# Making the Strassen operands of x inside the buffers that the first group multiplies from

## The chip, the cores and the metric

The kernel runs on one core of a Trainium2 chip. The metric is the device time of one execution in microseconds (us); three runs of the kernel before took 867.95, 872.8 and 872.8 us, median 872.8. Engines are named as in the profile: PE (TensorE), DVE (VectorE), ACT (ScalarE), POOL (GpSimd), SP (SyncE, which issues DMAs).

## The reference

```python
def _attn_ref(q, k, v):                       # q, k, v: (4, 8, 576, 64) float32
    gamma = 1.0 - 2.0 ** (-5.0 - np.arange(H))
    Dmat = np.where(rel >= 0, gamma[:, None, None] ** rel, 0.0)     # rel = i - j
    return np.matmul(scale * np.matmul(q, k.transpose(0, 1, 3, 2)) * Dmat, v)
def _moe_ref(x, w_in, w_out):                 # w_in (512, 2048), w_out (2048, 512)
    h = x @ w_in
    return np.maximum(0.01 * h, h) @ w_out
def _moe2_ref(x, w_in, w_out):
    h = np.maximum(x @ w_in, 0.0)
    return h * h @ w_out
# reference: x = attention, turned to (2304, 512); then _moe_ref; then _moe2_ref
```

## The kernel before, in words

**Attention stage.** 2304 tokens are worked through as 20 chunks (four batches of five; the fifth of each is half a chunk). Per chunk PE makes the scores, DVE multiplies them by the decay mask (tile `r`, L465), PE makes the output and a running state, and ACT copies both (L506, L509). The outputs go to three tiles `ysb`, one for each block of 768 tokens. Between chunks the program issues a few steps of two other jobs: making weights (`run`, counts in `RATE`) and making operands of x (`build`, counts in `BUILD`).

**Two feed-forward layers.** A layer is four groups of 512 hidden columns (`g` = 0 to 3; below, groups 0 to 3 are layer 0, groups 4 to 7 are layer 1). A group goes over the three blocks of tokens (`p` = 0 to 2), so there are 24 blocks, called (group, p). A block has a first half, `first`: seven products a la Strassen (`product`, L274, 12 matmuls each) of weight operands with operands of x; and a second half, `second`: the product with w_out (L371), 96 matmuls in layer 0 and 72 in layer 1. Around them ACT copies PSUM (tile `s`, L300), DVE adds (L322, L336, L341), and each result is split into a rounded part (`ghi`, ACT, L307) and the rest (`glo`, DVE, L312), since one float32 matmul is made of three on rounded parts. The results of `second` are copied to `ysb` by ACT in a layer's first group (L380), and added to it by DVE in the others (L382).

**Weights.** They are prepared a group ahead: 40 steps a group (two tasks of 12 steps for w_in, two of 8 for w_out), each step one or two instructions, nearly all on DVE, on tiles `raw` and `sf`. `raw` has one buffer, loaded by SP in two DMAs (`ahead`, L111); a task begins on ACT with `exponent` (L120), which waits for that load. `pace` is called between products and sets how many steps are issued where; one unit of its clock `now` is one product, 15 to a block.

**Operands of x.** A block's seven products need seven combinations of quarters of `ysb`, each as a rounded part (ACT, L227) and the rest (DVE, L233). `operands(layer, p)` makes them with 4 subtractions on DVE (L239 to L245), and ACT's queue stores both parts to DRAM (L205). `load_x` loads them from DRAM on SP's queue (L260) into five buffers `x` (`SLOTS`), for every group. Only the first five of block (0, 0) are made in the buffers themselves. In layer 0 the operands are made in the attention stage and in block (0, 0); for layer 1, `operands(1, p)` is made in the block after (3, p).

The order of instructions on each engine is the order in which the program emits them. All engines take theirs in order.

Of the kernel before, what the change touches and what calls it, by code (L numbers as in the profile page):

```python
# [19 lines left out]
P = 128  # L20
# [6 lines left out]
HT = 384  # L27
# [22 lines left out]
def retention_ffn_kernel(ctx: ExitStack, tc: tile.TileContext, full, rows, half, halfv, w1, w2, const, mask, gk, out):  # L50
# [40 lines left out]
    class Weights:  # L91


        def __init__(self):
            self.tasks = []
            for g in range(2 * NG):
                layer, f = divmod(g * GRP, NF)
                a, b, c, d = ((j, layer, f + 2 * u) for j in range(2) for u in range(NU))

                self.tasks += [a, c, d, b] if g else [a, b, c, d]  # L100
            self.raws, self.loads = [], 0

        def ahead(self):

            if self.loads < len(self.tasks):
                j, layer, f = self.tasks[self.loads]
                raw = stage.tile([P, 2, DM, 2], U32, tag="raw", bufs=RAW, name="raw")
                for i in range(2):

                    src = (w1, w2)[layer][f + i if j else f + 1 - i, j]  # L110
                    nc.sync.dma_start(raw[:, i].rearrange("p n t -> p (n t)"), src)  # L111
                self.raws.append(raw.rearrange("p i n t -> p (i n) t"))
                self.loads += 1

# [7 lines left out]
        def steps_in(self, layer, f):  # L122
# [17 lines left out]
            yield  # L140
            nc.vector.tensor_tensor(v, v, t, add)  # L141
            yield

            self.ahead()
# [17 lines left out]
        def steps_out(self, layer, f):  # L162
# [18 lines left out]
            yield  # L181
            nc.scalar.activation(hi, f32(a), AF.Copy)
            yield
            self.ahead()
# [17 lines left out]
    late = []  # L202

    def store(dst, src):
        nc.scalar.dma_start(f32(dst.rearrange("p k n -> p (k n)")), f32(src.rearrange("p k n -> p (k n)")))  # L205

    def flush():

        while late:
            layer, p, i, x, lo = late.pop(0)  # L210
            store(x[:, 1], lo)
            xd[layer, p, i] = x

    def operands(layer, p):

        x = ysb[p].rearrange("p (k t n) -> p k t n", k=NK, t=2)
        b11, b21, b12, b22 = (x[:, k : k + 2, t] for t in range(2) for k in (0, 2))

        def put(i, src):
            x = dram.tile([P, 2, 2, HT], F32R, name=f"x{layer}{p}{i}")  # L220
            if (layer, p) == (0, 0) and i < SLOTS:

                t = xs[0, 0, 0, i] = xpool.tile([P, 2, 2, HT], F32R, tag="x", name="x")
                hi, lo = t[:, 0], t[:, 1]
            else:
                hi = stage.tile([P, 2, HT], F32R, tag="xb", bufs=XB, name="xb")
            nc.scalar.activation(hi, src, AF.Copy)  # L227
            store(x[:, 0], hi)
            flush()
            yield  # L230
            if (layer, p) != (0, 0) or i >= SLOTS:
                lo = stage.tile([P, 2, HT], F32R, tag="xb", bufs=XB, name="xb")
            nc.vector.tensor_tensor(lo, src, f32(hi), sub)  # L233
            late.append((layer, p, i, x, lo))
            yield

        yield from put(0, b11)
        yield from put(1, b21)
        nc.vector.tensor_tensor(b11, b12, b11, sub)  # L239
        yield from put(6, b22)  # L240
        nc.vector.tensor_tensor(b12, b22, b12, sub)
        yield from put(4, b11)
        nc.vector.tensor_tensor(b22, b22, b11, sub)
        yield from put(3, b12)
        nc.vector.tensor_tensor(b21, b21, b22, sub)  # L245
        yield from put(2, b22)
        yield from put(5, b21)
        flush()

    uses = [(l, g, p, i) for l in range(2) for g in range(NG) for p in range(NB) for i in range(7)]  # L250
    loaded, used = [SLOTS], [0]
# [265 lines left out]
    def run(n, limit):  # L517

        while n > 0 and done[0] < limit:
            next(steps, None)  # L520
            done[0] += 1
            n -= 1

    def build(n=1):

        ran = 0
        while builds and ran < n:
            try:
                next(builds[0])
                ran += 1  # L530
            except StopIteration:
                builds.pop(0)
# [3 lines left out]
    with tc.manual_schedule():  # L536
        with tc.tile_pool(name="att", bufs=1) as pool, tc.tile_pool(name="ps_s", bufs=1, space=PSUM) as ps_s:
# [20 lines left out]
            for i in range(n):  # L558
# [12 lines left out]
                for p in range(NB):  # L571
                    a, t = tokens(i)
                    if a < (p + 1) * 2 * HT <= a + t:
                        builds.append(operands(0, p))
# [12 lines left out]
        run(GROUP, GROUP - OWN)  # L587


        whole = NB * 15  # L590
        for layer in range(2):
            for g in range(NG):
# [15 lines left out]
                built = [0]  # L608
                for p in range(NB):

# [11 lines left out]
                    if layer == 0 and g == NG - 1:  # L622
                        builds.append(operands(1, p))
# [56 lines left out]
```

## Time and profile before

| | |
|---|---|
| runs | 867.95, 872.8, 872.8 us |
| the profiled execution: its time, its span | 871.71 us, 869.9 us |
| PE busy, DVE busy, ACT busy, POOL busy | 834.7, 602.6, 343.4, 47.4 us |
| attention stage, up to the first product | 103.76 us |
| a block where PE never waits | 31.2 us (layer 0), 30.95 us (layer 1) |
| mean granted TensorE clock | 0.980 of full speed |

The profile gives, for each engine, the time in which it was busy. A view by stretches gives the same for a window of time; the length of the window stands first in its row. For a block of the feed-forward layers the window runs from its first matmul to that of the next block, so its length is the block's time.

### The profile page before, as it was taken

The numbers are of one execution on the slowest core, as the hardware profiler recorded it, in microseconds if no ns is written. First come the engines' busy times: TensorE is split into PE (matmuls) and PEld (weight loads), VectorE is DVE, ScalarE is ACT, GpSimd is POOL, SyncE is SP. The second block draws the span as 40 slices with busy tenths as digits, with TensorE's granted clock in tenths as the row PEclk, the third lists the DMA queues.
The fourth block names the chain that finished last, engine by engine and source line by source line (L and its number), as shares of the span: only waits on it lengthen the run. The fifth ranks groups of instructions, "written<-read, shape, count | busy, mean of one in ns | idle before, by whom it ended". The sixth has DMA issues, their size and how long they took to land.

```text
span 869.9 us, 12551 instructions
## 1 busy us (share of the span) xinstructions
PE 834.7 (96%) x5084; PEld 785.2 (90%) x5084; DVE 602.6 (69%) x734; ACT 343.4 (39%) x447; POOL 47.4 (5%) x36
## 2 busy tenths in 40 slices
PE   8868899999999999999998999999999999999998
PEld 7767799999999999999998988789989988998996
DVE  3898776555776576667778888576778688755534
ACT  2444565455354245235345445343333223321311
POOL 2647000000000000000000000000000000000000
PEclk9988699999999999999999999999999999999999
DMA  9999699575486467457579897766558547735831
GB/s 338 312 360 353 248 379 347 191 297 204 159 298 250 150 247 271 180 202 302 178 320 386 329 375 284 259 238 254 169 230 302 190 159 281 268 107 209 284 136 72
DMA packets 57065, 220.12 MB, mean 253 GB/s; under 512 B 6960, under 2 KB 7984, under 8 KB 57008
## 3 DMA queue, kind: packets, MB, share of 16 engines
q1 hardware_dynamic: 44912, 186.29, 58.4%
q10 hardware_dynamic: 12096, 33.04, 9.8%
q8 instruction: 40, 0.66, 0.3%
q14 instruction: 17, 0.14, 0.0%
HBM read 181.55 MB, written 37.75 MB: 252 GB/s over the span
## 4 chain that ended last, share of the span: by engine, by line
PE 74%; DVE 11%; DMA 8%; ACT 3%; issue 2%; ACTq 0%; SPq 0%; POOL 0%; DVEq 0%; POOLq 0%
PE yps L371 40%; PE a L274 20%; PE b L274 14%; DMA raw<-in_w 4%; DMA gq<-in_const 2%; DMA x<-x 1%; DVE r L465 1%; DVE xb L233 1%; DVE sf L180 1%; ACT t L283 1%; DMA mask<-in_mask 1%; ACT sf L120 1%; DMA x<-xb 1%; ACT ghi L307 1%; DVE sf L141 1%
## 5 line engine op out<-in xcount | busy, mean ns | idle before, releaser
L274 PE MATMUL a<-x,ihi 128*128 128x384 f32 x768 | 197.2, 337 | 4.5 <-ACT s L300 2.8
L274 PE MATMUL b<-x,ihi 128*128 128x384 f32 x576 | 147.0, 336 | 3.7 <-DVE t L322 2.7
L274 PEld LDWEIGHTS a<-x,ihi 128*128 128x128 f32 x768 | 139.6, 189 | 7.4 <-ACT s L300 4.1
L371 PE MATMUL yps<-ghi,ohi 128*128 128x384 f32 x384 | 128.7, 335 | 1.6 <-ACT ysb L380 0.5
L274 PE MATMUL a<-x,ilo 128*128 128x384 f32 x384 | 129.3, 337 | 0.0
L371 PE MATMUL yps<-glo,ohi 128*128 128x384 f32 x384 | 128.4, 334 | 0.6 <-DVE glo L312 0.6
L371 PE MATMUL yps<-ghi,olo 128*128 128x384 f32 x384 | 128.3, 334 | 0.0
L312 DVE TENSOR_TENSOR glo<-t,ghi 128x768 fp32r<-128x768 f32 x96 | 91.8, 956 | 47.6 <-ACT ghi L307 46.8
L382 DVE TENSOR_TENSOR ysb<-yps,ysb 128x384 f32<-128x384 f32 (+1 forms) x126 | 75.8, 610 | 62.8 <-PE yps L371 62.4
L371 PE MATMUL yps<-ohi,glo 128*128 128x512 f32 x288 | 112.3, 390 | 0.0
L371 PE MATMUL yps<-olo,ghi 128*128 128x512 f32 x288 | 112.3, 390 | 0.0
L371 PE MATMUL yps<-ohi,ghi 128*128 128x512 f32 x288 | 112.0, 389 | 0.0
L274 PEld LDWEIGHTS b<-x,ihi 128*128 128x128 f32 x576 | 103.9, 188 | 5.4 <-DVE t L322 3.3
L307 ACT ACTIVATE ghi<-t 128x768 fp32r<-128x768 f32 x96 | 81.1, 845 | 68.8 <-DVE t L285 55.4
L300 ACT ACTIVATE s<-a 128x768 f32<-128x768 f32 x48 | 39.0, 812 | 153.3 <-PE a L274 151.2
L274 PE MATMUL b<-x,ilo 128*128 128x384 f32 x288 | 96.3, 334 | 0.0
L371 PEld LDWEIGHTS yps<-ghi,ohi 128*128 128x128 f32 x384 | 72.1, 188 | 2.8 <-DVE ysb L382 1.1
L371 PEld LDWEIGHTS yps<-glo,ohi 128*128 128x128 f32 x384 | 72.1, 188 | 0.8 <-DVE glo L312 0.8
L274 PEld LDWEIGHTS a<-x,ilo 128*128 128x128 f32 x384 | 72.7, 189 | 0.0
L371 PEld LDWEIGHTS yps<-ghi,olo 128*128 128x128 f32 x384 | 72.1, 188 | 0.0
L322 DVE TENSOR_TENSOR t<-b,s 128x768 f32<-128x768 f32 x24 | 23.0, 956 | 70.2 <-PE b L274 64.0
L371 PEld LDWEIGHTS yps<-ohi,glo 128*128 128x128 f32 x288 | 54.1, 188 | 11.3
(63 smaller groups left out, 1049.3 us busy)
## 6 DMA issues: line engine op xcount, KB each, us to landing
x<-x SPq DMA_DIRECT2D x163, 768.0 KB, 6.0
raw<-in_w SPq DMA_DIRECT2D x64, 512.0 KB, 6.2
x<-xb ACTq DMA_DIRECT2D x74, 384.0 KB, 6.8
kv<-in_rows SPq DMA_DIRECT2D x16, 512.0 KB, 6.7
out<-ysb SPq DMA_DIRECT2D x18, 256.0 KB, 2.0
q<-in_full SPq DMA_DIRECT2D x16, 256.0 KB, 5.5
kt<-in_full SPq DMA_DIRECT2D x16, 256.0 KB, 5.5
x<-x ACTq DMA_DIRECT2D x10, 384.0 KB, 6.1
```

What stands on the lines that cost most here:

```text
L120: nc.scalar.activation(f32(a), f32(raw[:, :, 1]), AF.Abs)
L141: nc.vector.tensor_tensor(v, v, t, add)
L180: nc.vector.scalar_tensor_tensor(a, high, 1 << 31, a, ALU.bitwise_and, ALU.bitwise_or)
L233: nc.vector.tensor_tensor(lo, src, f32(hi), sub)
L274: nc.tensor.matmul(ps[:, u, :HT], a[:, w, s], x[:, b, k], start=(start and k == 0 and i == 0), stop=(k == 1 and i == 2), skip_group_check= ...
L283: nc.scalar.activation(t, src, AF.Prelu, alpha=0.01)
L300: nc.scalar.activation(t, ps[:, :, :HT], AF.Copy)
L307: nc.scalar.activation(h, t, AF.Copy)
L312: nc.vector.tensor_tensor(l, t, f32(gs[key][0]), sub)
L322: nc.vector.tensor_tensor(t11, b[:, :, :HT], s1, add)
L371: nc.tensor.matmul(acc, a, b, start=(j == u == i == 0), stop=(j == 1 and u == NU - 1 and i == 2))
L382: nc.vector.tensor_tensor(y, acc, y, add)
```

## The change

Seven buffers `x` stand in place of five, and the staging buffers `xb` are gone. The operands of a layer's first group are made in these buffers, in the order of use, and that group multiplies from them without a load; each is stored to DRAM whole, on SP's queue, from the same buffer (`store`, called from `pace`), and only groups 1 to 3 of a layer load them. So `operands(layer, p + 1)` is built in the second half of block (first group, p), `operands(1, 0)` in that of block (3, 2), and only `operands(0, 0)` in the attention stage. A difference that was written over b22 has a tile of its own (`t2`). The last 8 weight steps of the first group (`OWN`) move from the attention stage into block (0, 0). `ahead` is called one step earlier, and in the groups a weight task does not begin before three units of `pace` have gone by since its load was emitted (`ARRIVE`). The paces of groups 0, 3 and 4 are set by a share for each block (`SHARE`) in place of an exponent.

```diff
-SLOTS = 5
+SLOTS = 7
-XB = 5
-RATE = [1, 2, 2, 3, 3, 3] + [2] * 13 + [0]
-BUILD = [0] * 6 + [2] * 13 + [0]
+RATE = [1, 1, 2, 2, 2, 2] + [2] * 11 + [0] * 3
+BUILD = [0] * 6 + [1] * 11 + [0] * 3
-SPACE = 0.9
-BEND = {0: 1.6, NG - 1: 0.7, NG: 1.4}
-OWN = 0
+SPACE = .65
+SHARE = {0: (0.15, 0.45), NG - 1: (0.47, 0.85), NG: (0.2, 0.55)}
+OWN = 8
+LAG = 1
+ARRIVE = 3
...
         def steps(self):
             for j, layer, f in self.tasks:
+                while self.clock < self.due:
+                    yield True
                 yield from (self.steps_out if j else self.steps_in)(layer, f)
...
+    def store(use, x):
+        layer, _, p, i = use
+        d = dram.tile([P, 2, 2, HT], F32R, name=f"x{layer}{p}{i}")
+        nc.sync.dma_start(f32(d.rearrange("p a k n -> p (a k n)")), f32(x.rearrange("p a k n -> p (a k n)")))
+        xd[layer, p, i] = d
...
+        def hi(i, src):
+            use = layer, 0, p, i
+            while uses[loaded[0]] != use or loaded[0] == used[0] + SLOTS:
+                yield True
+            loaded[0] += 1
+            xt[i] = xs[use] = xpool.tile([P, 2, 2, HT], F32R, tag="x", name="x")
+            nc.scalar.activation(xt[i][:, 0], src, AF.Copy)
+        def lo(i, src):
+            t = xt[i]
+            nc.vector.tensor_tensor(t[:, 1], src, f32(t[:, 0]), sub)
+            kept.append(((layer, 0, p, i), t))
+        yield from hi(0, b11)
+        yield
+        yield from hi(1, b21)
+        lo(0, b11)
+        yield
+        lo(1, b21)
         nc.vector.tensor_tensor(b11, b12, b11, sub)
+        yield
+        nc.vector.tensor_tensor(t2, b22, b11, sub)
+        yield
+        yield from hi(2, t2)
...
-            if (l, p, i) not in xd:
+            if g == 0 or (l, p, i) not in xd:
                 break
...
+        weights.arrive = ARRIVE
...
                 def pace(now, ceiling):
-                    part = min(1, now / (whole - 3)) ** BEND.get(i, 1)
+                    into = min(1, (now - 15 * p) / (6 if busy[p] else 12 if p == NB - 1 else 15))
+                    share = (0, *SHARE.get(i, (0.36, 0.71)), 1)
+                    part = share[p] + (share[p + 1] - share[p]) * into
                     want = start + math.ceil((limit - start) * part)
-                    if builds and now >= built[0]:
-                        build()
-                        built[0] = now + SPACE
+                    while len(kept) > LAG:
+                        store(*kept.pop(0))
+                    while builds and now >= built[0] and build():
+                        built[0] = max(built[0], now - 1) + SPACE
+                    if not builds:
+                        while kept:
+                            store(*kept.pop(0))
+                    weights.clock = whole * i + now
...
                 for p in range(NB):
+                    built = [15 * p + 8]
+                    if g == 0 and p + 1 < NB:
+                        builds.append(operands(layer, p + 1))
+                    elif layer == 0 and g == NG - 1 and p == NB - 1:
+                        builds.append(operands(1, 0))
...
                     second(layer, g, p, gs, in_second)
-                    if layer == 0 and g == NG - 1:
-                        builds.append(operands(1, p))
+                    build(99)
+                weights.due = 0
+                run(GROUP, limit)
```

DVE near the end of the attention stage, from one full chunk's mask product (`r`) to the last, before (`ysb_67` is the second block of x):

```order
L465 TENSOR_TENSOR r<-scps,mask 128x1024
L172 TENSOR_SCALAR raw<-raw 128x1024
L239 TENSOR_TENSOR ysb_67<-ysb_67 128x2x384
L174 TENSOR_SCALAR sf<-sf 128x1024
L233 TENSOR_TENSOR xb<-ysb_67,xb 128x768
L465 TENSOR_TENSOR r<-scps,mask 128x1024
L176 SCALAR_TENSOR_TENSOR sf<-raw 128x1024
L241 TENSOR_TENSOR ysb_67<-ysb_67 128x2x384
L178 TENSOR_SCALAR sf<-sf 128x1024
L233 TENSOR_TENSOR xb<-ysb_67,xb 128x768
L465 TENSOR_TENSOR r<-scps,mask 64x8x64
```

and the same chunks of the change:

```order
L483 TENSOR_TENSOR r<-scps,mask 128x1024
L183 SCALAR_TENSOR_TENSOR sf<-raw,sf 128x1024
L234 TENSOR_TENSOR x<-ysb_66,x 128x768
L483 TENSOR_TENSOR r<-scps,mask 128x1024
L188 TENSOR_SCALAR sf<-sf 128x1024
L234 TENSOR_TENSOR x<-ysb_66,x 128x768
L190 SCALAR_TENSOR_TENSOR olo<-sf 128x1024
L483 TENSOR_TENSOR r<-scps,mask 64x8x64
```

Eight instructions stand between these three mask products before, five in the change; the operands of the second block are gone from the stage, and so is the last weight task (L172, L174 and so on).

SP's DMAs of the change from the end of the attention stage into block (0, 1) (`x_1028` and so on are the DRAM copies; L211 stores, L113 loads raw weights):

```order
L113 DMA raw<-in_w 128x1024 x2
L211 DMA x_1028<-x 128x1536
L211 DMA x_1030<-x 128x1536
L211 DMA x_1032<-x 128x1536
L211 DMA x_1034<-x 128x1536
L211 DMA x_1036<-x 128x1536
L211 DMA x_1038<-x 128x1536
L113 DMA raw<-in_w 128x1024 x2
L211 DMA x_1203<-x 128x1536
```

Six stores of whole operands stand one behind the other ahead of a load of raw weights. Before, SP's queue had seven loads of x in their place, and the stores were on ACT's queue, two halves for each operand.

DVE of the change in the last building block, (4, 1), from the third-last sum of its first half (`t_4778` is the difference's own tile):

```order
L359 TENSOR_TENSOR t<-b,s 128x768
L303 SCALAR_TENSOR_TENSOR t<-t 128x768
L330 TENSOR_TENSOR glo<-t,ghi 128x768 x2
L306 TENSOR_TENSOR t<-t 128x768
L330 TENSOR_TENSOR glo<-t,ghi 128x768
L234 TENSOR_TENSOR x<-ysb_68,x 128x768
L188 TENSOR_SCALAR sf<-sf 128x1024
L190 SCALAR_TENSOR_TENSOR olo<-sf 128x1024
L234 TENSOR_TENSOR x<-ysb_68,x 128x768
L244 TENSOR_TENSOR ysb_68<-ysb_68 128x2x384
L175 TENSOR_SCALAR raw<-raw 128x1024
L177 TENSOR_SCALAR sf<-sf 128x1024
```

Before, the operands of layer 1 were made in blocks (3, 1), (3, 2) and (4, 0); here those of the third block stand in (4, 1), among its weight steps.

## Rows read from the trace of the kernel before

**Rows 1.** The page: span, busy time by engine, granted clock by fortieths.
```profile
span 869.9 us, 12551 instructions
PE 834.7 (96%) x5084; PEld 785.2 (90%) x5084; DVE 602.6 (69%) x734; ACT 343.4 (39%) x447; POOL 47.4 (5%) x36
PEclk9988699999999999999999999999999999999999
```
**Rows 2.** Windows: each block that waits, two groups that don't; length first.
```profile
core 0: us, PE busy (x) PEld busy (x) DVE busy (x) ACT busy (x) POOL busy (x), PEclk, DMA share, GB/s
...
103.76:137.08 33.32, 33.32 (x181) 33.32 (x182) 21.74 (x26) 17.73 (x25) 0.00 (x0) 0.93 0.91 346
137.08:170.09 33.01, 31.77 (x181) 31.13 (x181) 20.97 (x25) 19.05 (x26) 0.00 (x0) 1.00 0.77 286
170.09:203.76 33.67, 32.06 (x182) 31.17 (x182) 18.57 (x22) 16.43 (x23) 0.00 (x0) 1.00 0.60 227
203.76:297.36 93.60, 93.60 (x542) 93.60 (x542) 60.77 (x82) 37.57 (x44) 0.00 (x0) 1.00 0.60 222
...
390.96:423.20 32.24, 31.50 (x182) 31.18 (x182) 24.20 (x33) 13.77 (x16) 0.00 (x0) 1.00 0.63 237
423.20:455.66 32.46, 31.96 (x182) 31.09 (x182) 23.09 (x28) 15.93 (x19) 0.00 (x0) 1.00 0.75 288
455.66:489.94 34.28, 32.10 (x182) 31.14 (x182) 30.89 (x43) 17.07 (x21) 0.00 (x0) 1.00 0.98 384
489.94:521.31 31.37, 31.16 (x157) 28.03 (x157) 25.40 (x32) 14.44 (x19) 0.00 (x0) 1.00 0.92 347
521.31:553.53 32.22, 31.23 (x157) 28.06 (x156) 21.67 (x24) 14.80 (x19) 0.00 (x0) 1.00 0.81 292
553.53:587.40 33.87, 31.76 (x158) 28.03 (x156) 25.39 (x30) 16.01 (x21) 0.00 (x0) 1.00 0.60 226
...
587.40:680.24 92.84, 92.84 (x470) 84.30 (x469) 70.86 (x88) 30.25 (x35) 0.00 (x0) 1.00 0.61 224
```
**Rows 3.** Timeline of block (0, 2): SP's raw load, ACT behind it, PE's stall.
```profile
177.01 0.93 SPq L111 DMA_DIRECT2D raw<-in_w  x2
...
184.96 1.12 ACT L120 ACTIVATE sf<-raw 128x1024 f32<-128x1024 f32 x1 [5.53 <-DMA raw<-in_w]
...
189.49 0.44 PE L371 MATMUL yps<-ghi,ohi 128*128 128x384 f32 x1 [0.52 <-ACT ghi L307]
```
**Rows 4.** Windows of the attention stage: sixth to twentieth mask product, and the rest.
```profile
25.91:97.02 71.11, 56.63 (x768) 49.92 (x768) 65.17 (x62) 32.75 (x59) 37.39 (x25) 0.83 0.92 331
97.02:103.76 6.74, 4.38 (x52) 3.75 (x49) 6.74 (x9) 4.85 (x9) 0.00 (x0) 0.82 0.72 251
```
**Rows 5.** The same first window, DVE and ACT on ysb alone (operands, copies).
```profile
25.91:97.02 71.11, 20.10 (x17) 16.40 (x27) 0.83 0.92 331
```
**Rows 6.** DVE and ACT on sf alone: attention, one w_out task, one group.
```profile
25.91:97.02 71.11, 31.25 (x29) 8.32 (x8) 0.83 0.92 331
...
167.20:179.30 12.10, 5.58 (x6) 1.06 (x2) 1.00 0.46 150
203.76:297.36 93.60, 30.02 (x36) 10.52 (x10) 1.00 0.60 222
```
**Rows 7.** Timeline, DVE near the end of the attention stage.
```profile
89.47 0.69 DVE L172 TENSOR_SCALAR raw<-raw 128x1024 uint32<-128x1024 uint32 x1 [1.64 <-DMA raw<-in_w]
```
**Rows 8.** Groups by form, whole span: busy, mean ns, idle before and its causes.
```profile
L312 DVE TENSOR_TENSOR glo<-t,ghi 128x768 fp32r<-128x768 f32 x96 | 91.8, 956 | 47.6 <-ACT ghi L307 46.8
...
L382 DVE TENSOR_TENSOR ysb<-yps,ysb 128x384 f32<-128x384 f32 x72 | 38.9, 552 | 25.8 <-PE yps L371 25.6
L382 DVE TENSOR_TENSOR ysb<-yps,ysb 128x512 f32<-128x512 f32 x54 | 37.0, 687 | 36.9 <-PE yps L371 36.8
L233 DVE TENSOR_TENSOR xb<-ysb,xb 128x768 fp32r<-128x768 f32 x37 | 36.9, 997 | 10.0 <-ACT xb L227 7.7 <-DMA x<-xb 2.3
```
**Rows 9.** DMA issues: KB each, median us from issue to landing.
```profile
raw<-in_w SPq DMA_DIRECT2D x64, 512.0 KB, 6.2
```

More of the change, by code (lines that the diff above doesn't have):

```diff
@@ L101, in __init__ @@
             self.raws, self.loads = [], 0
+            self.clock, self.due, self.arrive = 0, 0, 0
         def ahead(self):
@@ L113, in ahead @@
                 self.loads += 1
+                self.due = self.clock + self.arrive
         def exponent(self, a, raw):
@@ L140, in steps_in @@
             yield
+            self.ahead()
             nc.vector.tensor_tensor(v, v, t, add)
             yield
-            self.ahead()
             a21, a22, a11, a12, s1, s2, s3, s4 = (sf[:, i] for i in range(8))
@@ L181, in steps_out @@
             yield
+            self.ahead()
             nc.scalar.activation(hi, f32(a), AF.Copy)
             yield
-            self.ahead()
             nc.vector.tensor_single_scalar(a, a, 0xFF800000, ALU.bitwise_and)
@@ L200, in retention_ffn_kernel @@
     xs = {}
[L202 to L212, printed above, removed]
+    def store(use, x):
[3 more added lines that the diff above has]
+        xd[layer, p, i] = d
+    kept = []
     def operands(layer, p):
@@ L217, in operands @@
         b11, b21, b12, b22 = (x[:, k : k + 2, t] for t in range(2) for k in (0, 2))
[L219 to L235, printed above, removed]
@@ L237, in operands @@
-        yield from put(0, b11)
-        yield from put(1, b21)
+        t2 = stage.tile([P, 2, HT], F32, tag="t2", name="t2")
+        xt = {}
+        def hi(i, src):
[9 more added lines that the diff above has]
+            kept.append(((layer, 0, p, i), t))
@@ L246, in operands @@
-        yield from put(2, b22)
-        yield from put(5, b21)
-        flush()
+        yield
+        yield from hi(3, b12)
+        lo(2, t2)
+        yield
+        yield from hi(4, b11)
+        nc.vector.tensor_tensor(b21, b21, t2, sub)
+        yield
+        yield from hi(5, b21)
+        lo(3, b12)
+        yield
+        yield from hi(6, b22)
+        lo(4, b11)
+        yield
+        lo(5, b21)
+        yield
+        lo(6, b22)
+        yield
     uses = [(l, g, p, i) for l in range(2) for g in range(NG) for p in range(NB) for i in range(7)]
-    loaded, used = [SLOTS], [0]
+    loaded, used = [0], [0]
@@ L519, in run @@
         while n > 0 and done[0] < limit:
-            next(steps, None)
+            if next(steps, None):
+                break
             done[0] += 1
@@ L528, in build @@
             try:
-                next(builds[0])
+                if next(builds[0]):
+                    break
                 ran += 1
@@ L570, in retention_ffn_kernel @@
                 att.output(i)
[L571 to L574, printed above, removed]
+                a, t = tokens(i)
+                if a < 2 * HT <= a + t:
+                    builds.append(operands(0, 0))
                 run(1, GROUP - OWN)
@@ L599, in pace @@
                 def pace(now, ceiling):
-                    part = min(1, now / (whole - 3)) ** BEND.get(i, 1)
+                    into = min(1, (now - 15 * p) / (6 if busy[p] else 12 if p == NB - 1 else 15))
+                    share = (0, *SHARE.get(i, (0.36, 0.71)), 1)
+                    part = share[p] + (share[p + 1] - share[p]) * into
                     want = start + math.ceil((limit - start) * part)
-                    if builds and now >= built[0]:
-                        build()
-                        built[0] = now + SPACE
+                    while len(kept) > LAG:
[6 more added lines that the diff above has]
+                    weights.clock = whole * i + now
                     if now % 15 not in (6, 8):
                         run(min(2, max(want, start if now > 1 else 0) - done[0]), ceiling)
-                built = [0]
+                busy = [g == 0] * (NB - 1) + [layer == 0 and g == NG - 1]
                 for p in range(NB):
+                    built = [15 * p + 8]
[3 more added lines that the diff above has]
+                        builds.append(operands(1, 0))
                     def in_first(m):
```

5 lines of the change are left out of this document (removed).

## The prediction, made before the changed kernel was run

> **What bounds the kernel now.** I read the page first [rows 1]: PE is busy 834.7 of 869.9 us, so only time in which PE waits, or runs at the lower clock, can be gained. The windows by block show where that is [rows 2]. The groups at 203.76 and 587.40 take 93.60 and 92.84 us with PE busy throughout: 31.2 us a block in layer 0, 30.95 in layer 1, the floor. The nine other rows stand over it by 2.12, 1.81, 2.47 (group 0), 1.04, 1.26, 3.08 (group 3), 0.42, 1.27 and 2.92 us (group 4), together 16.4 us. The first is clock and not waiting: PE is busy all 33.32 us, at a mean granted clock of 0.93, since it starts at the lower level (1.2 GHz). The other blocks run at 1.00, and their excess is waiting. All are groups in which operands of x are made, stored or loaded for the first time, and no other group waits.
>
> The timeline of block (0, 2) shows the pattern of such a wait [rows 3]. SP issues a load of raw weights at 177.01, between loads of x; ACT reaches `exponent` and stands idle 5.53 us until 184.96; `ghi`, behind it in ACT's queue, comes late, and PE stalls at 189.49.
>
> The attention stage is the rest: 103.76 us. From the sixth mask product to the last [rows 4] DVE is busy 65.17 of 71.11 us, PE 56.63, and the mean clock is 0.83. DVE is the bound there, PE next. Before 25.91 us the stage waits for its inputs, which do not change, so I cost the first 25.91 us at nothing.
>
> **Attention stage, work removed.** By the order of instructions, the stretch 25.91 to 97.02 holds 17 operand instructions on DVE before and 11 after; on `sf` 29 before and 27 after; of L172 on `raw` two before and one after. At this stretch's own means these are 6 x 20.10/17 = 7.1 us [rows 5], 2 x 31.25/29 = 2.2 us and 0.7 us [rows 6, 7], together 10.0 us. From below: if PE, with its own 14.5 us of waiting, holds the pace, the gain is 0. From above: it can't pass 71.11 - 56.63 = 14.5 us unless the clock rises. I take 10.0, since DVE's 65.17 is the nearest to the stretch. DVE's 5.94 us of idle time I leave as it is, though some of it hangs on the raw load [rows 7] that now comes earlier.
>
> After the last mask product, DVE works all 6.74 us before; afterwards none of that work is there, and what remains is PE's 4.38 and ACT's, of 4.85 [rows 4]. The gain lies between 0 and 2.4 us; I take 1.5. ACT also loses its store issues there, which I cost at nothing. Attention: **-11.5 us**, the first product at about 92.
>
> **Groups, stalls removed.** In the first group of a layer there are no loads of x any more: 42 loads of 0.79 MB, less five already made in place. In (3, 2) DMA ran at 384 GB/s with a share of 0.98 [rows 2], as stores of x and loads for the next group fell together; now that block only stores. A task now begins three units after its load is emitted: 3 x 31.2/15 = 6.2 us, the median landing [rows 9]. So the waits behind `exponent` should go.
>
> **Groups, work moved in.** Each build costs DVE 11 instructions at 0.997 us, 11 us [rows 8]. It lies in the second half of a block, after that half's operands are ready. A steady group of layer 0 keeps DVE busy 60.77 us [rows 2]; group 0 has no additions on DVE (24 x 0.552 = 13.2 us, on ACT as before) but two builds (22 us) and the 8 late weight steps (5.58 + 0.7 us [rows 6]): 60.8 - 13.2 + 22 + 6.3 = 75.9 of 93.6 us. Group 3: 60.8 + 11 = 71.8. Group 4: 70.86 - 18 x 0.687 + 22 = 80.5 of 92.8. So there is cover in every group, and what counts is single blocks. Four places are left:
> - (0, 0) starts after a stretch of mixed clock, as before: 2.1.
> - (0, 1): a raw load is emitted behind six stores, and `exponent` stands in ACT's queue ahead of part of the operands. Six stores are 4.7 MB, at 384 GB/s 12.3 us; the load is emitted about four products after the first store, some 8 us, and `exponent` is reached some 8 us later. That delays DVE by 2 to 3 us, of which two products' slack hides 1 to 2: 1.0.
> - (3, 2): the operands alternate with additions that free PSUM for PE; three operand or weight instructions (3.1 us) stand between the first two additions: 0.6.
> - (4, 1): from its first sum to that of the next block DVE has 11 instructions of its own at 0.956 [rows 8], 11 operand instructions at 0.997, and 13 weight steps at 30.02/36 = 0.83 [rows 6]: 10.5 + 11.0 + 10.8 = 32.3 us against 30.95: 1.4.
>
> Left over: 5.1 of 16.4 us. Groups: **-11.3 us**. Bounds: at best only the 2.1 of the clock stays, -14.3; at worst each of the five building blocks waits as (4, 2) did before, 2.9 us, so 14.5 + 2.1 stay and nothing is gained.
>
> **Nothing elsewhere.** The other groups have the same DVE order as before, with x loaded two products earlier; their x came in time already. The stores move from ACT's queue to SP's; ACT was busy 343 us [rows 1], so its issue time buys nothing.
>
> **Sum.** 871.71 (the profiled execution, 1.1 below the median of the runs shown) - 11.5 - 11.3 = **849 us**.
>
> **Rivals.**
> 1. PE takes over the attention stage. Its 56.63 us of work at a clock of 0.83 is near the 61 us that DVE would need, and a PE that waits for each mask product stays at the lower level for part of the time. Then only the groups gain: 871.7 - 11.3 = 860. For it: the 0.83. Against it: DVE is busy longer than PE there, and the DMA engines (share 0.92) lose the stores.
> 2. The raw loads come late behind whole stores. Stores and raw loads now stand in one queue, in order; 4.7 MB ahead of a load put it 12.3 us back, twice what `ARRIVE` allows. If the wait that cost (0, 2) its 2.47 us [rows 2, 3] occurs at five of the eight raw loads of groups 0 and 4, that is 12 us, the groups' gain is gone, and 871.7 - 11.5 = 860 is left. The Trainium skill (DMA: Bandwidth & Descriptors, on queues, rings and completion order) says that each DMA engine takes turns between the queue rows that have work, SP and ACT owning one row each. By that rule a raw load before shared the engines with ACT's stores half and half, and would now wait for all of them: it speaks for this rival; no row here shows the turns. Against it: (0, 0) alone has six stores in a burst, elsewhere they come one by one as DVE finishes them.
> 3. Slower: each rest of an operand (DVE) waits for its rounded part (ACT). Before, four such waits took 7.7 us, 1.9 each [rows 8]. With 7 in a build, all of 1.9, a building block would need 13 us more of DVE. The five blocks' sums are now, by the same count as for (4, 1), about 28.5, 26.8, 27.9, 29.0 and 32.3 against 31.2 (the first three) and 30.95; they would be 10.6, 8.9, 10.0, 11.4 and 14.7 late, 56 us: 871.7 - 11.5 - 14.3 + 56 = 902. It decides from about 1.05 us a wait: with 7.4 us more in each block the late ends sum to the 25.8 us of both gains. Against it: a rounded part is emitted a step ahead of its rest, with other work between.
> 4. Both gains come out small: attention 3 to 5, groups 3 to 4, within 1% of before, 865.
>
> **Chances.** The forecast 0.60 (own range 842 to 858), rival 1 0.17, rival 2 0.10, rival 3 0.05, rival 4 0.08. A measurement of this kernel can tell about 1%. Faster by more: the first three, 0.87; within 1%: 0.08; slower: 0.05. The range takes in the forecast's best bounds (14.5 + 2.4 + 14.3 = 31 us, 840.5, and a few us more if the clock in the attention stage rises) and rivals 1 and 2 with the few us by which runs differ: 837 to 863.
>
> **What would show it.** The first product at 88 to 96 us, with DVE still over 85% busy from the sixth mask product on (if PE is busy over 95% there, rival 1). Blocks (0, 2), (3, 0), (3, 1) and (4, 2) at 31.2 and 30.95 us; (4, 1) the longest of layer 1. Idle time of ACT before `exponent` in the groups of a few us in all; if it is 5 us at a time beside stores, rival 2. DVE waiting for ACT before operands over 1 us each would be rival 3. I am wrong on the main term if the first product comes after 99 us.

## The result, and the profile after

The changed kernel takes **847.84 us** (median of four runs, 846.42 to 849.14) against 872.16 us for the kernel before in the same comparison (four runs, 867.95 to 872.8): a ratio of 0.9731, 95% interval 0.9694 to 0.9767. Forecast were 849 us and a range of 837 to 863. The profiled execution took 849.14 us, 22.57 less than that of before, which went into the sum; the medians differ by 24.3.

The page after, in the lines of [rows 1] and those on DMA:

```profile
span 847.4 us, 12380 instructions
PE 826.2 (98%) x5084; PEld 779.8 (92%) x5084; DVE 602.8 (71%) x734; ACT 340.5 (40%) x447; POOL 46.5 (5%) x36
...
PEclk9998999999999999999999999999999999999999
...
DMA packets 45688, 191.01 MB, mean 225 GB/s; under 512 B 5696, under 2 KB 6720, under 8 KB 45632
...
x<-x SPq DMA_DIRECT2D x168, 768.0 KB, 6.1
raw<-in_w SPq DMA_DIRECT2D x64, 512.0 KB, 5.1
```

DVE does as many instructions as before, 734, and is busy as long, 602.8 us for 602.6: nothing was saved on it, its work was moved to places where PE does not wait for it. The DMAs carry 191.01 MB (the page before says 220.12), and a raw load lands in 5.1 us for 6.2 [rows 9].

The windows after: the attention stage from the sixth mask product to the last, the rest of it (both answer to [rows 4]), and from 92.39 on the blocks of [rows 2] in the same order; each window is a block, from its first matmul to that of the next.

```profile
core 0: us, PE busy (x) PEld busy (x) DVE busy (x) ACT busy (x) POOL busy (x), PEclk, DMA share, GB/s
26.20:88.45 62.25, 53.74 (x771) 47.30 (x772) 57.04 (x53) 28.96 (x55) 36.48 (x25) 0.92 0.70 245
88.45:92.39 3.94, 3.05 (x47) 2.61 (x45) 1.38 (x3) 1.83 (x5) 0.00 (x0) 1.00 1.01 417
92.39:124.19 31.80, 31.71 (x181) 31.29 (x182) 24.24 (x28) 19.36 (x26) 0.00 (x0) 1.00 0.60 230
124.19:156.68 32.49, 31.50 (x182) 31.16 (x181) 26.77 (x33) 22.06 (x33) 0.00 (x0) 1.00 0.54 199
156.68:188.91 32.23, 31.78 (x182) 31.14 (x182) 22.41 (x28) 16.16 (x23) 0.00 (x0) 1.00 0.91 370
...
376.11:407.31 31.20, 31.20 (x182) 31.20 (x182) 23.90 (x33) 13.89 (x16) 0.00 (x0) 1.00 0.62 228
407.31:438.50 31.19, 31.19 (x181) 31.19 (x181) 21.46 (x29) 11.94 (x14) 0.00 (x0) 1.00 0.63 228
438.50:470.23 31.73, 31.72 (x181) 31.14 (x181) 23.88 (x32) 16.12 (x20) 0.00 (x0) 1.00 0.33 128
470.23:501.15 30.92, 30.92 (x157) 28.08 (x157) 27.57 (x34) 15.67 (x21) 0.00 (x0) 1.00 0.56 209
501.15:533.63 32.48, 31.36 (x157) 28.06 (x156) 27.30 (x34) 18.18 (x24) 0.00 (x0) 1.00 0.48 175
533.63:564.80 31.17, 31.17 (x158) 28.06 (x156) 26.76 (x31) 15.26 (x22) 0.00 (x0) 1.00 0.93 358
```

The first product comes at 92.39 for 103.76: **-11.4 us**. The long stretch of the attention stage fell from 71.11 to 62.25 us (-8.9), its tail from 6.74 to 3.94 (-2.8), and 0.3 were lost up to the sixth mask product. In the stretch DVE has 57.04 us of work for 65.17 and is still busy 92% of the time; PE is busy 86%, at 0.92 of full speed for 0.83. Over the floor of 31.2 and 30.95 us the nine blocks now stand by 0.60, 1.29, 1.03, 0, 0, 0.53, 0, 1.53 and 0.22, together 5.2 us for 16.4: **-11.2 us**. The sum, -22.6, is the whole difference of the profiled times.

One execution stands behind each of these figures. The attention stage is the same program in seven of the kernels below (after, e2, e4, e7, e9, e9b, e10): in their profiled executions its long stretch took 60.6 to 63.0 us and the first product came at 91.89 to 94.22. A difference of some 2 us at the start, taken by itself, says nothing.

### The profile page after: what moved, and what is told of

The parts are those of the page before. It is cut to its first block, busy times and chain, and to the rows that moved or that the text cites. A ratio compares the mean times of both kernels' runs of the same rounds, so it can differ in the third digit from the quotient of the medians.

```text
span 847.4 us, 12380 instructions
## 1 busy us (share of the span) xinstructions
PE 826.2 (98%) x5084; PEld 779.8 (92%) x5084; DVE 602.8 (71%) x734; ACT 340.5 (40%) x447; POOL 46.5 (5%) x36
## 2 busy tenths in 40 slices
DMA packets 45688, 191.01 MB, mean 225 GB/s; under 512 B 5696, under 2 KB 6720, under 8 KB 45632
## 4 chain that ended last, share of the span: by engine, by line
PE 86%; DVE 6%; DMA 5%; ACT 2%; SPq 1%; issue 1%; DVEq 0%; ACTq 0%
PE yps L389 46%; PE a L292 21%; PE b L292 16%; DMA kt<-in_full 1%; DMA x<-x 1%; DMA raw<-in_w 1%; PE scps L481 1%; PE ops L509 1%; DMA kv<-in_rows 1%; PE ops L512 1%; DVE r L483 1%; ACT sf L123 1%; DVE sf L179 1%; DVE t L340 0%; DVE sf L183 0%
## 5 line engine op out<-in xcount | busy, mean ns | idle before, releaser
L389 PEld LDWEIGHTS yps<-ohi,glo 128*128 128x128 f32 x288 | 54.1, 188 | 11.2
L389 PEld LDWEIGHTS yps<-olo,ghi 128*128 128x128 f32 x288 | 54.1, 188 | 11.0
```

The lines of the kernel that those rows point to most:

```text
L389: nc.tensor.matmul(acc, a, b, start=(j == u == i == 0), stop=(j == 1 and u == NU - 1 and i == 2))
```

## Experiments

Times are medians; a ratio is to the kernel before on the same chip. "More than the kernel after" is the difference to 847.84 us, and so across chips on which the kernel before had medians of 870 to 872. "Excess" is a block's time over its floor, as above, for all blocks but the last, which has none behind it. A "throttled stretch" is one at the lower granted clock.

| run | us | ratio, 95% | first product | excess of the first 23 blocks |
|---|---|---|---|---|
| before | 872.16 | | 103.76 | 16.4 |
| after | 847.84 | 0.9694 to 0.9767 | 92.39 | 5.2 |
| e5_dve_work_back | 859.85 | 0.9823 to 0.9908 | 101.81 | 6.8 |
| e1_weights_back | 852.93 | 0.9753 to 0.982 | 95.71 | 6.9 |
| e6_store_traffic_back | 855.88 | 0.9782 to 0.9866 | 97.88 | 7.2 |
| e11_store_traffic_on_sp | 853.12 | 0.9769 to 0.9821 | 96.30 | 7.2 |
| e8_all_back | 864.22 | 0.9887 to 0.9945 | 105.36 | 6.4 |
| e2_no_arrive | 860.86 | 0.9855 to 0.9917 | 91.89 | 17.1 |
| e3_arrive_alone | 870.02 | 0.9969 to 1.0013 | 105.60 | 12.6 |
| e4_stores_on_act | 855.88 | 0.9797 to 0.985 | 93.18 | 11.0 |
| e7_fewer_steps_first_half | 861.26 | 0.9831 to 0.993 | 93.30 | 19.7 |
| e9_spread_steps | 851.52 | 0.9746 to 0.9801 | 92.28 | 7.9 |
| e9b_spread_steps_less | 848.09 | 0.9704 to 0.9762 | 93.82 | 3.6 |
| e10_longer_delay | 849.46 | 0.9721 to 0.9779 | 94.22 | 5.4 |

### What sets the pace of the attention stage

**DVE's work put back.** Ten subtractions of the operands' shape (128 x 768), whose result nobody reads, into DVE's stream in chunks 13 to 17:

```diff
+                if 12 <= i <= 16:
+                    y = ysb[0].rearrange("p (k t n) -> p k t n", k=NK, t=2)[:, 0:2, 0]
+                    t = stage.tile([P, 2, HT], F32, tag="t2", name="t2")
+                    for _ in range(2):
+                        nc.vector.tensor_tensor(t, y, y, sub)
```

> The change with ten idle subtractions of 128x768 on VectorE in chunks 13 to 17 of the attention stage, about as many as the operand instructions of the second block that left it; no stores. Theory (VectorE's work sets the pace): 10 x 0.95 to 1.2 us, less some of the 5.2 us in which VectorE is idle there: first product 6 to 10 us later, at 98 to 102, total 854 to 858. Rival (what counted were the stores): 0 to 2 us, 848 to 850.

The windows of this kernel, sixth to last mask product, then the tail, then block (0, 0):

```profile
25.53:98.13 72.60, 55.00 (x792) 48.30 (x792) 69.77 (x64) 30.36 (x58) 39.25 (x25) 0.93 0.66 235
98.13:101.81 3.68, 2.48 (x25) 2.22 (x25) 1.28 (x3) 0.38 (x1) 0.00 (x0) 0.70 1.02 426
101.81:135.46 33.65, 33.65 (x181) 33.38 (x182) 24.24 (x28) 19.47 (x26) 0.00 (x0) 0.93 0.46 173
```

DVE's busy time rises by 12.7 us against the kernel after, the stretch by 10.4, and the first product comes 9.4 us later. PE's waits for the mask product rise from 7.1 to 15.7 us. DVE does set the pace here, as forecast. The total, 859.85, lies above the theory's 854 to 858: block (0, 0) takes 1.85 us more, with PE busy throughout at a mean clock of 0.93: it again begins at the lower level, and that adds to what work in the attention stage costs.

**The weight steps put back.** `RATE` and `OWN` as before, so that the eight steps run in the attention stage:

```diff
-RATE = [1, 1, 2, 2, 2, 2] + [2] * 11 + [0] * 3
+RATE = [1, 2, 2, 3, 3, 3] + [2] * 13 + [0]
-OWN = 8
+OWN = 0
```

> The change with OWN = 0 and the old RATE: all 40 weight steps of the first group are in the attention stage again. Theory (DVE sets the pace of the attention stage): the 8 steps, 7 instructions and 6.3 us on DVE, come back in full, first product at 98 to 100 us instead of 92.4, and at most 1 us of it returns in blocks (0, 0) and (0, 1), which get lighter: 852.5 to 855. Rival (TensorE or the transfers set the pace there): first product at 92 to 94, total 847 to 849.

The first product comes at 95.71, 3.3 us later and less late than expected, and the groups' excess is 1.7 us larger; nothing came back in the groups for the steps that left them. With the groups' part the kernel loses 5.1. The total is in the theory's range, but by another way than the theory's. DVE has 58.68 us of work in the stretch for 57.04, and the stretch takes 60.92 us for 62.25. What grew is the tail, 8.04 us for 3.94, and PE fills it (104 matmuls for 47):

```profile
87.67:95.71 8.04, 6.99 (x104) 6.05 (x104) 3.74 (x4) 4.93 (x11) 2.36 (x1) 1.00 0.64 193
```

PE had fallen behind earlier, as it waited for `kt`, the keys of a chunk (timeline of SP and PE):

```profile
72.64 1.79 SPq L113 DMA_DIRECT2D raw<-in_w  x2
...
74.96 0.42 SPq L455 DMA_DIRECT2D kt<-in_full  x1
...
80.84 2.08 PE L481 MATMUL scps<-q,kt 64*128 64x128 f32 x16 [6.54 <-DMA kt<-in_full]
```

With the old `RATE` a raw load stands ahead of the last loads of `kt` in SP's queue. It goes out when DVE has read the one `raw` buffer (L183, until 72.57), and the load of `kt` goes out behind it; in the kernel after all loads of `kt` are out before this raw load. So the 3.3 us, 1.5 more than the latest of the seven equal stages, do not answer to the 2.2 + 0.7 that the prediction had counted for these steps on DVE, and no run measures those by themselves. A like wait of PE, 6.66 us until 60.95, stands in the kernel before in the middle of the stretch; DVE's next mask product, at 61.20, followed there without idle time.

**The stores put back.** 26 stores of 384 KB, half an operand each, from the first buffer `x`, in chunks 8 to 20, once on ACT's queue and once on SP's:

```diff
+                if i >= 7:
+                    for j in range(2):
+                        d = dram.tile([P, 2 * HT], F32R, name=f"spare{i}{j}")
+                        nc.scalar.dma_start(f32(d), f32(xs[0, 0, 0, 0][:, 0].rearrange("p k n -> p (k n)")))
```

> The change with 26 stores of half operands (384 KB each, all of the same finished half) on ACT's queue in chunks 8 to 20 of the attention stage, as many as before; no work on VectorE. Theory (VectorE sets the pace): 0 to 2 us, first product at 92 to 94.5. Rival (the stores, on the DMA engines or in ACT's queue, set it): 5 to 9 us, first product at 97 to 101.

The windows with the stores on ACT's queue, and then ACT at the end of the stage (its DMA issues are the rows ACTq) and PE's first product:

```profile
26.18:88.50 62.32, 51.87 (x768) 45.82 (x768) 57.66 (x54) 28.50 (x54) 35.45 (x24) 0.95 0.99 358
88.50:97.88 9.38, 4.38 (x53) 3.80 (x49) 1.37 (x3) 2.47 (x6) 0.00 (x0) 0.74 1.02 419
```

```profile
94.30 3.09 ACTq L603 DMA_DIRECT2D spare<-x  x2
97.44 0.38 ACT L527 ACTIVATE ysb<-ops 128x256 f32<-128x256 f32 x1 [3.98 <-DMA x<-x]
...
97.88 1.01 PE L292 MATMUL a<-x,ihi 128*128 128x384 f32 x2 [2.99 <-ACT ysb L527]
```

The stretch is as long as without the stores (62.32 us for 62.25), though the DMA engines' share went from 0.70 to 0.99. What grew is the tail, 9.38 us for 3.94: the last copy of attention output, on which the first product waits, stands in ACT's queue behind two issues that take 3.09 us, and PE waits 2.99 us for it (0.47 in the kernel after). A copy of the state behind an earlier issue costs PE 1.85 us for 0.42, and PE's own work takes 4.38 us for 3.05, at 0.74 of full speed for 1.00. Block (0, 0) then loses 2.0 us at the lower clock. So stores on ACT's queue do cost in the attention stage, by 8.0 us in all, as the rival had it, where the prediction had put them at nothing.

With the same stores issued by SP (`nc.sync.dma_start` in the line above):

> The 26 added half-stores of e6_store_traffic_back (384 KB each, chunks 8 to 20 of the attention stage), issued on SP's queue and not on ACT's. What e6 showed: the last mask product came at 88.50 as without the stores (88.45), the DMA engines' share rose from 0.70 to 0.99, and the first product came 5.5 us later because ACT's last copy stood behind two issues of 3.1 us. Theory (it is the issues on ACT's queue that cost, not the traffic): the first product at 92 to 94 us, group 0 without throttled stretch, 847.5 to 850.5 us. Rival (the traffic itself costs, now also by raw loads that come behind stores in SP's queue): DVE waits for raw loads 4 us or more in all from the sixth mask product on, the first product at 96 us or later, 853 to 858 us.

```profile
25.57:91.51 65.94, 54.19 (x766) 47.85 (x768) 57.50 (x53) 28.32 (x54) 36.09 (x25) 0.90 0.92 333
91.51:96.30 4.79, 3.74 (x55) 3.09 (x51) 1.37 (x3) 2.65 (x6) 0.00 (x0) 1.00 1.03 410
```

Neither expectation holds as it stands. The tail is short again (4.79 us), which is the theory's part: the 9.38 was ACT's issues. But the last mask product comes 3.1 us later than in the kernel after, and the time lies between both (853.12). The rival's mechanism is not what did it: up to the first product DVE waits for a raw load once, for 0.26 us. Of the 3.7 us by which the stretch is longer, 1.9 have gathered by the eleventh mask product, 5 us after the first added store; without added stores six equal stages also lose 0.6 to 1.4 us there against the kernel after. The rest comes at the sixteenth, where PE waits for a load of `kt` and DVE for PE's scores:

```profile
68.32 2.08 PE L481 MATMUL scps<-q,kt 64*128 64x128 f32 x16 [4.02 <-DMA kt<-in_full]
...
70.44 1.23 DVE L483 TENSOR_TENSOR r<-scps,mask 128x1024 f32<-128x1024 f32 x1 [1.68 <-PE scps L481]
```

A `kt` load takes 6.6 us to land for 5.8 in the kernel after, and PE waits for `kt` four times, 6.7 us in all, where it never does in the kernel after. But in the six other kernels with that stage it waits 0.6 to 4.7 us. So what the traffic by itself costs stays open.

On the two queues, the Trainium skill (DMA: Bandwidth & Descriptors, "Queues, rings and completion order") says that a DMA engine takes turns between the queue rows that have work. By that, moving the stores into SP's row should have put `kt` loads behind them. The measured medians are 6.9 us with the stores in ACT's row and 6.6 in SP's own: here it made no difference that shows.

**All three put back**, the edits of e1, e5 and e6 in one kernel:

> The change with all three put back into the attention stage: the 8 weight steps and old RATE, the ten subtractions on VectorE, the 26 stores. If these three are what left the stage, the first product is back at 102 to 106 us (before: 103.76). If VectorE alone counts, the stores add nothing over the sum of the other two; if the parts hide one another, the sum of the three single delays is larger than this one.

The first product comes at 105.36, that of before at 103.76. The three single costs at the start, 3.3 + 9.4 + 5.5, sum to 18.2 us, together they cost 13.0; in the medians 25.1 and 16.4. Parts of them hide one another.

### What took the stalls out of the groups

**The delay taken away**: a weight task may begin as soon as its load is emitted.

```diff
-ARRIVE = 3
+ARRIVE = 0
```

> The change with ARRIVE = 0: a weight task may begin as soon as the pace wants it, whether its load has landed or not. Theory (the delay is what took the waits behind the exponent away): ACT waits of 3 to 6 us for raw loads come back in groups 0, 3 and 4, with 1 to 3 us of TensorE each, 851 to 855. Rival (the waits went because loads of x and half stores no longer share the engines with raw loads): 847 to 849.

The timeline of block (4, 2) in this kernel: SP's raw load, ACT's wait for it, and PE:

```profile
544.11 1.90 SPq L113 DMA_DIRECT2D raw<-in_w  x2
...
555.70 1.12 ACT L123 ACTIVATE sf<-raw 128x1024 f32<-128x1024 f32 x1 [9.50 <-DMA raw<-in_w]
...
561.21 0.79 PE L389 MATMUL yps<-ohi,ghi 128*128 128x512 f32 x1 [5.55 <-ACT ghi L325]
```

and the same load in the kernel after, with ACT between it and its use:

```profile
541.20 1.61 SPq L113 DMA_DIRECT2D raw<-in_w  x2
...
547.22 0.85 ACT L325 ACTIVATE ghi<-t 128x768 fp32r<-128x768 f32 x1 [3.93 <-DVE t L303]
...
553.81 1.12 ACT L123 ACTIVATE sf<-raw 128x1024 f32<-128x1024 f32 x1 [1.12 <-DMA raw<-in_w]
```

This is the pattern of [rows 3]: `exponent` waits for the load at the head of ACT's queue, and three `ghi` behind it come late. In both kernels the load needs some 12 us; in one ACT does the `ghi` first. The block loses 8.7 us without the delay, 0.2 with it: PE's wait of 5.55 us, and a throttled stretch from 559.8 to 566.6 that it brings. The kernel loses 13.0 us, more than the theory had; of the 11.4 between the profiled executions 8.5 stand in (4, 2), 3.0 in (0, 0), half of that as lower clock in its first half, and 0.7 in (3, 1). But (0, 2) and (3, 2), which had lost 2.47 and 3.08 us before, stand at 0.77 and 0.51 without the delay too.

**The delay without the rest**: the kernel before, with the delay, and with the raw loads emitted a step earlier (against the kernel before):

```diff
+ARRIVE = 3
...
+                self.due = self.clock + self.arrive
...
+                while self.clock < self.due:
+                    yield True
```

> The kernel before with the delay of weight tasks and the earlier call of ahead alone, operands as before. Theory (delay): blocks (0, 2), (3, 2) and (4, 2) lose most of their 8.5 us, 864 to 868. Rival (the crowded queue did it): the raw loads still come late, by 7 to 8 us from issue, and 870 to 873 remains.

870.02 us, no gain that can be measured. The excess fell from 16.4 to 12.6 us (block (0, 2) to 0), but (4, 2) still loses 3.9 us and the first product comes at 105.60. So neither part by itself gives the groups' gain: 12.6 us are left with the delay alone and 17.1 with the operands alone, 5.2 with both. The new paces (`SHARE`) came with the operands, and what they do was not tested apart.

**The stores on ACT's queue**, one line of the kernel after changed:

```diff
-        nc.sync.dma_start(f32(d.rearrange("p a k n -> p (a k n)")), f32(x.rearrange("p a k n -> p (a k n)")))
+        nc.scalar.dma_start(f32(d.rearrange("p a k n -> p (a k n)")), f32(x.rearrange("p a k n -> p (a k n)")))
```

> The change with its stores on ACT's queue instead of SP's. Theory (the burst of six stores is harmless either way, as DMA is not the limit): 847 to 850, the first block after it within 0.5 us. Rival (stores ahead of a raw load in one queue delay it): the raw load emitted in block (0, 0) lands 3 to 6 us sooner after its issue, and block (0, 1) loses its 1.3 us; 846 to 847, unless the issues hold ACT up by as much.

8.0 us more, which neither range foresaw, though the rival had named the way. Block (0, 0) has 6.5 of the 6.7 us by which the profiled executions differ; its timeline on ACT (and ACT's DMA issues), DVE and PE:

```profile
95.73 5.74 ACTq L211 DMA_DIRECT2D x<-x  x6
101.57 1.12 ACT L123 ACTIVATE sf<-raw 128x1024 f32<-128x1024 f32 x1 [5.04 <-issue]
...
102.72 0.69 DVE L177 TENSOR_SCALAR sf<-sf 128x1024 f32<-128x1024 f32 x1 [12.21 <-ACT sf L123]
...
104.34 1.01 PE L292 MATMUL b<-x,ihi 128*128 128x384 f32 x2 [4.62 <-DVE t L340]
```

Six issues hold ACT for 5.74 us; `exponent` behind them, the weight step on DVE that waits for it, the sum behind that step and PE follow in turn, and PE's clock is at the lower level from 102.1 to 108.9. In the kernel after the same `exponent` runs at 95.63. There SP had issued these six stores at 84.31, in the attention stage, since nothing in its own queue held it back (timeline of SP and ACT; the last row is `exponent` of the next raw load, without a wait):

```profile
84.31 5.45 SPq L211 DMA_DIRECT2D x<-x  x6
101.41 0.81 SPq L113 DMA_DIRECT2D raw<-in_w  x2
...
111.61 1.12 ACT L123 ACTIVATE sf<-raw 128x1024 f32<-128x1024 f32 x1
```

The Trainium skill (DMA: Bandwidth & Descriptors, "Issuing engines are not separate DMA queues") calls the time that a sequencer takes to initiate a DMA "usually small relative to the DMA itself". The trace agrees for each of them: 0.96 us on ACT, where the median from issue to landing is 6.1 us in the kernel after. Six in a row on a computing engine took 5.74 us of its queue, and block (0, 0) 6.5.

### What is left in the groups

In (0, 1) and (4, 1) PE waits once, for the sum at L354. For (4, 1), DVE of the kernel after from the sum at L340 to that at L354, for which PE then waits 1.12 us (the other two instructions between them are left out):

```profile
505.61 0.96 DVE L340 TENSOR_TENSOR t<-b,s 128x768 f32<-128x768 f32 x1 [3.44 <-PE b L292]
...
507.48 2.09 DVE L161 TENSOR_TENSOR ilo<-sf,ihi 128x768 fp32r<-128x768 f32 x2
509.48 0.69 DVE L175 TENSOR_SCALAR raw<-raw 128x1024 uint32<-128x1024 uint32 x1
510.81 0.69 DVE L177 TENSOR_SCALAR sf<-sf 128x1024 f32<-128x1024 f32 x1 [0.64 <-ACT sf L123]
...
512.28 1.22 DVE L179 SCALAR_TENSOR_TENSOR sf<-raw 128x1024 uint32<-128x1024 uint32 x1
513.42 0.69 DVE L181 TENSOR_SCALAR sf<-sf 128x1024 uint32<-128x1024 uint32 x1
514.02 0.95 DVE L354 TENSOR_TENSOR t<-a,s 128x768 f32<-128x768 f32 x1
```

Six weight steps stand between the two sums. DVE had idled 3.44 us just before, so it is not the block that is too full, as the prediction had it, but this place. In (0, 1) L161 stands there twice too, each waiting for ACT's `ihi` (0.98 and 1.42 us), then L175 and L177, and PE loses 1.29.

**At most one step at a time in the first halves:**

```diff
-SHARE = {0: (0.15, 0.45), NG - 1: (0.47, 0.85), NG: (0.2, 0.55)}
+SHARE = {0: (0.15, 0.45), NG - 1: (0.47, 0.85), NG: (0.2, 0.5)}
-                        run(min(2, max(want, start if now > 1 else 0) - done[0]), ceiling)
+                        most = 1 if g == 0 and p and now % 15 < 6 else 2
+                        run(min(most, max(want, start if now > 1 else 0) - done[0]), ceiling)
```

> The change with at most one weight step at a time (instead of two) in the first halves of the second and third block of a layer's first group, and a share of 0.5 instead of 0.55 after two blocks of group 4. Theory (the waits left in (0, 1) and (4, 1), 1.3 and 1.5 us, are weight steps that stand between two sums of the first half): both go to 0.3 or less, (0, 2) keeps up to 1, total 844.5 to 846.5. Rival (VectorE is overfull over the whole block): the wait moves to the next block's start, 847 to 849.

The two waits are gone (both first halves at their floor), and the kernel is 13.4 us slower, outside both ranges: (0, 1) loses 4.0 us in its second half, and the next groups' first blocks 5.9 and 8.5. PE waits 2.1, 2.6 and 5.7 us there, and each time a throttled stretch begins, of 3.4, 6.8 and 6.8 us. At the start of group 5 ACT, and then PE:

```profile
570.03 1.12 ACT L123 ACTIVATE sf<-raw 128x1024 f32<-128x1024 f32 x1 [5.67 <-DMA raw<-in_w]
...
578.04 1.01 PE L292 MATMUL a<-x,ihi 128*128 128x384 f32 x2 [5.09 <-ACT ihi L159]
```

The weights are late: with one `raw` buffer a task's load is emitted only when the task before is nearly through, and a task pushed back pushes back all that follow it in the group.

**The steps spread by hand**, with as many done at the end of the block as before, in two versions (3, 1, 1, 1, 3 and 3, 2, 1, 1, 3 steps in the first five places of a block):

```diff
+                        most = {1: 3, 2: 1, 3: 1, 4: 1, 5: 3}.get(now % 15, 2) if g == 0 and p == 1 else 2
-                        run(min(2, max(want, start if now > 1 else 0) - done[0]), ceiling)
+                        run(min(most, max(want, start if now > 1 else 0) - done[0]), ceiling)
```

> In the second pair of blocks of each layer's first group (blocks (0,1) and (4,1)), the weight steps per slot of the eviction loop are set by hand (3, 1, 1, 1, 3 in five slots, 2 elsewhere), so that fewer of them stand on VectorE between the two uses of a PSUM half; how many have run at the end of the pair is unchanged. Theory (what is left of PE's idle time in (0,1) and (4,1), 1.3 and 1.5 us, is this lump of steps ahead of one eviction): both fall to 0.5 or less and nothing comes in their place, 845 to 846.5 us. Rival (VectorE is simply full there, so the lump moves): the same 2.8 us stand at the next eviction or at the next block's start, 847 to 849 us.

> As the other kernel with steps set by hand, but only one slot lighter (3, 2, 1, 1, 3). Theory of the lump: (0,1) and (4,1) give back about half or more of 2.8 us, 845.5 to 847 us. Rival (VectorE is full): 847 to 849 us.

The first version removes both waits for L354, and new ones come: (0, 1) loses 4.7 us in its second half, where ACT's `ohi` waits 4.66 us for a weight step on DVE with copies of PSUM behind it, and (4, 2) 1.5; at 851.52 us it is outside both ranges. The second brings (0, 1) to 0 and (0, 2) to 0.5; (4, 1) keeps 1.8, now behind ACT:

```profile
508.57 1.18 ACT L123 ACTIVATE sf<-raw 128x1024 f32<-128x1024 f32 x1 [3.07 <-DVE ilo L161]
...
510.49 0.62 PE L292 MATMUL a<-x,ihi 128*128 128x384 f32 x2 [1.28 <-ACT s L318]
```

Its excess is the lowest of all, 3.6 us for 5.2, but its first product came at 93.82, late among the equal stages, and 848.09 us is no different from 847.84.

**A longer delay:**

```diff
-ARRIVE = 3
+ARRIVE = 4
```

> The constant of the delay between a raw load and the weight task that reads it is 4 for 3. Theory: the 3.2 us that ACT's exponent waits for its raw load in block (0,2), and the 0.7 us of PE behind them, go; the other blocks stay, 847 us. Rival (the tasks then end too late, and the next raw load with them, as when fewer steps ran in the first half): block (0,3) or the next group's first block waits for its weights, 850 us or more.

Block (0, 2) loses its 0.7 us as the theory said, and (0, 1) gets 1.9 us in its second half, for the 1.3 of its first, where `ohi` again waits for a DVE step (3.75 us) ahead of the copies. 849.46 us: nothing gained.

## Why the prediction was right

**DVE's work in the attention stage, -10.0.** Right in cause and nearly in size: the stretch lost 8.9 us, 8.1 of DVE's work and 0.7 of its idle time, and e5 shows the pace following DVE. **The tail, -1.5** was -2.8 and above my bound of 2.4: PE's waits there fell by the 1.5, but PE's own 4.38 us, which I took for what remains, shrank to 3.05, at 1.00 of full speed for 0.82. That the stage came to -11.4 for -11.5 is luck in part, as the two misses cancel.

**"Its issue time buys nothing"** is the step that failed, twice: six issues on ACT's queue cost block (0, 0) 6.5 us (e4), and half-stores on it in the attention stage lengthen the tail by 5.4 us (e6), where the same stores on SP's queue leave it at 4.79 (e11). I had set ACT's busy time of 343 us against the span; but an issue holds the order of the queue, and what counts is who stands behind it. The sum came out right in spite of it because the kernel made the move, and, it seems, because the stores' cost in the attention stage lay beside DVE's: DVE's work and the weight steps, put back one by one, cost 9.4 + 3.3 = 12.7 us at the start, as much as all of it with the stores (13.0, e8). What the issues cost in the kernel before itself was not measured; there the last copy, at 103.32, came behind two of them, of 0.81 us in all.

**The groups' stalls, -11.3** was -11.2. PE's waits behind `exponent` went as said, but less by the delay than I had it: (0, 2) and (3, 2) hardly need it, and what it takes away are stalls of (0, 0) and (4, 2) that the change would otherwise have had (e2). ACT's idle time for raw loads is now 20.8 us in six waits, the longest 4.8, for 34.7 in nine:

```profile
ACT sf L123 <- DMA raw<-in_w: 20.8, 6, 4.8
```

In groups 0, 3 and 4 it is 8.5 us in three waits, for 24.3 before; that is more than the few us in all which I had named as a sign, but PE stands behind one of them only, in (0, 2).

**What was left, 5.1** was 5.2, but by other shares. Of 2.1 us for the clock in (0, 0), 0.6 are there, and not by the clock: PE's last throttled stretch ends at 70.9, and it runs the whole block at full speed. The 1.0 of (0, 1) is 1.3, but not from a raw load behind six stores: these had been issued 8 us before the first product, the load at 101.41 had landed when ACT came to it at 111.61, and in e4, without the burst in SP's queue, (0, 1) keeps its 1.29. The 1.4 of (4, 1) is 1.5, from a lump of steps and not from a full block; and the same in (0, 1). (0, 2), forecast at the floor, keeps 1.0, 0.7 of it a small remainder of the old pattern (e10). (3, 2) is 0.5 for 0.6. So that the sum agrees is luck.

**The rivals.** PE took over nothing (86% busy, not over 95%). Raw loads behind whole stores cost at most the 0.7 us of (0, 2). Waits of DVE for rounded parts came to one, of 1.0 us, so nothing of the slower case:

```profile
DVE x L234 <- ACT x L230: 1.0, 1, 1.0
```

## What to carry to other kernels

Work that is only moved can be worth its whole length: look for the stage in which an engine sets the pace, and for one in which it idles. A DMA issue in a computing engine's queue is priced by what stands behind it in that queue, not by that engine's busy time; give issues to an engine with no other work. That engine's queue has an order too: in e1 a raw load that waited for its buffer held up a load of `kt` behind it on SP, and PE with it. And a consumer that waits for a load at the head of an in-order queue is best put off until the load has landed, but no later, where one buffer makes each load wait for the task before it.

## What the runs showed of the hardware

- Six stores of 768 KB in a row held ACT's queue for 5.74 us, 0.96 each. The same six on SP in the kernel after took 0.42, 0.43, 0.57, 0.98, 1.77 and 1.00 us, on ACT 0.34, 0.45, 0.96, 1.29, 1.28 and 1.27: in a row they grow longer on either queue. All 42 on SP took 0.32 to 1.77 us, the median 0.33.
- More DMA traffic in the attention stage, from a share of 0.70 (245 GB/s) to 0.99 (358 GB/s), left the length of the stretch that DVE bounds unchanged in e6 (62.25 and 62.32 us); in e11, at 0.92 and 333 GB/s, it was 3.7 us longer, 1.7 of them at one late load of `kt`.
- Block (0, 0) takes 1.7 to 2.6 us more than its floor in every run in which a throttled stretch reaches into it and PE does not wait (before, e1, e3, e5, e6, e8, e11), and 0.6 where none does (after, e7, e9, e9b, e10).
- A wait of PE can cost more than its own length: in (4, 2) of e2 a wait of 5.55 us brought a throttled stretch of 6.8 us, and the block lost 8.7 us.
